# One PSUM buffer for all banks, a smaller copy of K, shared weight tiles, and sums of G written to PSUM, in a kernel that fuses attention with a gated MLP

## The chip, the cores and the metric

The kernel runs on one core of a Trainium2 chip. The metric is device time in microseconds (us) of one execution, lower is better. Engines: PE (TensorE), DVE (VectorE), ACT (ScalarE), POOL (GpSimd), and SP, which here only issues DMAs.

## The reference

```python
# q, k, v: 8 batches x 8 heads x 576 positions x 64;  tau = 0.02
scores = q @ k.T / sqrt(64)
scores = where(scores >= max(scores) - tau, scores, -1e9)
attn = exp(scores - max(scores));  attn = attn / sum(attn)
x = attn @ v                        # as 4608 tokens x 512
gate = sigmoid(x @ w_gate)          # w_gate, w_val: 512 x 1536
out = (gate * (x @ w_val)) @ w_out  # w_out: 1536 x 512
```

The scores decide by a threshold what counts, so they are computed in nearly full precision: each operand of a fast matmul (type fp32r) is split into a high part (rounded) and a low part (the rest), and the products high-high, high-low and low-high are summed in PSUM.

## The kernel before

**Planning.** The program is not written in the order in which it runs. It records operations with an engine, a cost, a key (the due time) and the buffers that they use; `Plan.run` then plays the record through with these costs and emits each operation when its engine, its inputs and its buffers are free, lowest key first. So a buffer count, a gate or a cost changes the order on all engines. Each engine executes its part strictly in order.

**Attention.** Heads are taken in pairs (a batch has four, 32 in all, numbered 0 to 31; `Visit`). A pair has nine score tiles of 128 queries by 576 keys: four for each head and one that holds the last 64 queries of both. For a tile (`tile_steps`), PE writes the scores to PSUM (L713, before pair 4 in plain fp32, L705), DVE takes the negative maximum (L721) and the threshold (L730), ACT the exponential (L735), and DVE masks and sums the row (L738); PE transposes the 576 columns (`tp` L819, `lk` L832), ACT copies them to SBUF (L771), and PE multiplies by V (`av`, L855). All reads of a score tile are from PSUM, so it is held from the scores to the mask.

**The score operands** (`split_scores`). K is split into `k2` (high and low). For each head `kd` is a copy by DMA of both parts, put once on the head's own 64 rows and once on the other 64; `qd` has the high part of Q on the own rows and the low part on the others. A tile is then two matmuls of 128 rows by halves of 288 keys: `qd` with kd's high part gives high-high and low-high, and `qd` with kd's low part gives high-low (and a negligible low-low).

**PSUM.** There are eight banks of 512 fp32 columns. Before pair 4 three score tiles of two banks and two single banks are in use. Once the MoE work has begun (`active["moe"]`), two score tiles keep four banks, and four single banks (`b`) serve transposes and `av` (at most two) and MoE sums (at most two).

**MoE.** Tokens are worked on in blocks of 512: blocks 0 to 7 are the first 512 positions of the batches, block 8 all the leftover positions. Blocks 0, 1 and 2 are multiplied directly, beside the attention of later batches (`in_units`): a unit is 12 matmuls of 512 columns (`m`, L938), 24 units a block, 72 in all. Units and pairs are tied to each other by `RATE` (2.7 units a pair from pair 4 on): a pair waits for a unit (`held_by`), and a unit for a pair. The weights of a unit, 512 KB, come from DRAM (`wi`), for each block anew. Meanwhile POOL forms sums of the weights (`in_sums`, `out_sums`). ACT (tanh) and DVE (L918) make G, the gated product, in two slabs of 512 tokens a tile. G of the blocks 2 and 6 goes to DRAM and comes back (`ga`, `gd`, `gb`).

**The tail.** After the attention come, in this order: the output stage of blocks 0, 1, 2; the input products of the block pairs 3-4 and 5-6 (`in_two`, seven products in place of eight, chains `qa`, `qb`, `qc` in PSUM, L1148); the output stage of blocks 3, 4, 5; the input products of 7-8; the output stage of 6, 7, 8. An output stage (`out_three`) multiplies a 3 by 3 grid of G (three parts of the 1536 features, three blocks) by the weights with 15 products of 24 matmuls (`oc`, L1222), 360 in all. `ORDER` gives the products' order, `G_STEPS` the sums of G that they need: ("n", d, x, y, sign) writes the sum of slabs x and y to d, ("c", r, x) splits slab x for product r. Each step is done for four columns. A sum is a DVE TENSOR_TENSOR of two SBUF slabs (L1009). A split (`halves_of`) is a rounded copy by ACT (`gt`, L1061) and a subtraction for the low part (L1064), by POOL, DVE, POOL in turn (`G_LOW`). The products' PSUM results are added up by ACT (L1243) and DVE (`oa`, L1247). The operands of the next input products (`xb`, `xs_p`) are made in the same way.

Of the kernel before, what the change touches and what calls it, by code (L numbers as in the profile page):

```python
# [46 lines left out]
class Plan:  # L47
# [3 lines left out]
    IN_TURN = ("x", "xf", "kn", "qn", "k2", "q2", "kd", "qd", "vs", "p", "pt", "pl", "ptc")  # L51
# [7 lines left out]
    def __init__(self, pools, slots):  # L59
# [5 lines left out]
        self.taken, self.now = {}, 0.0  # L65
# [4 lines left out]
    def make(self, b):  # L70
        if b.place is not None:
            at = min(b.place)
            tag = f"{b.tag}{at}"
            return self.bank_pool(tag).tile(b.shape, b.dtype, tag=tag, name=b.name, bufs=1)
# [38 lines left out]
    def room(self, o):  # L113
# [5 lines left out]
        for (tag, cls), s in need.items():  # L119
            own[tag] = own.get(tag, 0) + len(s)  # L120
        for (tag, cls), s in need.items():
            if tag in self.ANY:
                if sum(max(0, len(self.vacant[t]) - own.get(t, 0)) for t in self.homes_of(tag)) < len(s) + o.leave:
                    return False
                lines = {}
                for b in s:
                    if b.line is not None:
                        lines.setdefault(b.line, []).append(b.turn)
                if any(sorted(v) != list(range(self.given.get(k, 0) + 1, self.given.get(k, 0) + 1 + len(v)))
                       for k, v in lines.items()):  # L130
                    return False
                continue
# [33 lines left out]
    def settle(self, bufs):  # L166
# [3 lines left out]
        for b in bufs:  # L170
            if b.tag not in ("s", "b"):
                continue
            for at in self.homes(b.tag):
                if not taken & at:
                    places[b] = at
                    taken |= at
# [7 lines left out]
    def run(self):  # L184
# [10 lines left out]
        while True:  # L195
# [39 lines left out]
            while events and events[0][0] <= now + 1e-9:  # L235
# [5 lines left out]
                else:  # L241
                    for b in x.bufs:
                        b.users -= 1
                        if not b.users and b.held:
                            self.live.pop(b, None)
# [22 lines left out]
    "kn": 1, "qn": 1, "k2": 1, "q2": 1, "kd": 3, "qd": 3, "vs": 3,  # L268
    "p": 3, "pc": 1, "sm": 8, "st": 16, "pt": 4, "pl": 2, "ptc": 1, "plc": 1, "xf": 2, "rb": 1, "x": 6, "g": 12,
# [46 lines left out]
RATE, SLACK, LEAP = 2.7, 3, 5  # L316

def LATE(b, hp):
# [3 lines left out]
KD_COST = 1.2  # L322
# [3 lines left out]
SUMS_IN, SUM_KEY, SUM_OUT = {1: (0,), 2: (1,)}, 300, 290  # L326
# [5 lines left out]
G_LOW = ("POOL", "DVE", "POOL")  # L332
# [47 lines left out]
def kernel(  # L380
# [70 lines left out]
    ahead = ExitStack()  # L451
    ps_more = ahead.enter_context(tc.tile_pool(name="ps_more", bufs=1, space=PSUM))
    warm = ps.tile([P, 2, SM], F32, tag="s0", name="warm", bufs=1)
    for i in range(WARM):
        nc.tensor.matmul(
            warm[:, i % 2, :P], ident, ident, is_transpose=True, start=True, stop=True, skip_group_check=True
# [3 lines left out]
    pools["s"], pools["b"] = (ps, 3), (ps, 4)  # L460
# [3 lines left out]
    class Both(Plan):  # L464
        def cap(self, tag, cls):
            if tag == "s" and active["moe"]:
                return 2 if cls is None else None
# [6 lines left out]
            return 2 if active["att"] else 4  # L474

        def homes(self, tag):
            if tag == "s":
                return [{0, 1}, {2, 3}] + ([] if active["moe"] else [{4, 5}])
            return [{6}, {7}] + ([{4}, {5}] if active["moe"] else [])

        def bank_pool(self, tag):
            if tag == "s4":
# [469 lines left out]
    def streamed(blk, tag=""):  # L952
        return lambda f, i: stream(
            wi_d[f, i], lambda: wi_d[f, i].t.rearrange("p z c f -> p (z c f)"), f"wi{blk}_{f}_{i}{tag}"
        )

# [482 lines left out]
```

## Time and profile before

| | |
|---|---|
| median of 3 runs | 1462.29 us (1460.71 to 1463.02) |
| the profiled execution's own time | 1457.04 us |
| its span, first to last instruction | 1454.9 us |
| PE busy | 1341.3 us, 92% |
| DVE, ACT, POOL busy | 1065.1, 742.9, 618.7 us |
| mean granted PE clock | 0.97 |
| moved by DMA | 338.12 MB |

Columns of the views are named where they are shown. A group's row gives busy time and mean duration of its instructions, then the idle time of the engine just before them and what ended it. Names are those of the program, with buffer numbers left out; L1009 is line 1009 of the kernel.

### The profile page before, as it was taken

How to read it: one execution, taken by the hardware profiler on the slowest of the kernel's cores; microseconds unless marked ns; L12 is line 12 of the kernel's file. 1: busy time of each engine (PE TensorE's matmuls, PEld its weight loads, DVE VectorE, ACT ScalarE, POOL GpSimd, SP SyncE). 2: the span in 40 equal slices, each digit the busy share in tenths (PEclk: the TensorE clock that was granted, in tenths of full speed). 3: DMA queues.
4: the chain of work that ended last, by engine and by line, in shares of the span. 5: the costliest groups of instructions: out<-in, count | busy, mean ns of one | idle time of the engine just before them, and what ended most of it. 6: DMA issues, size and time to landing. Idle time of an engine off the chain costs nothing.

```text
span 1454.9 us, 23511 instructions
## 1 busy us (share of the span) xinstructions
PE 1341.3 (92%) x8184; PEld 1083.1 (74%) x8184; DVE 1065.1 (73%) x1936; ACT 742.9 (51%) x1375; POOL 618.7 (43%) x530
## 2 busy tenths in 40 slices
PE   8989999899999899999987979999999969999978
PEld 5568877787787677777765767888888758888757
DVE  7888778877777667677787887576546986456983
ACT  8787666667676666676655533132113434113431
POOL 3557222645634743655634565011001766001762
PEclk9999999999999899999988989999999989999989
DMA  8689668998988989999995338575666628676634
GB/s 319 197 247 334 195 189 277 266 307 239 282 231 240 273 269 275 269 289 265 312 296 156 111 127 298 193 249 195 220 224 214 218 90 311 199 254 222 196 95 151
DMA packets 137284, 338.12 MB, mean 232 GB/s; under 512 B 25040, under 2 KB 35536, under 8 KB 137168
## 3 DMA queue, kind: packets, MB, share of 16 engines
q1 hardware_dynamic: 137024, 336.64, 74.3%
q8 instruction: 65, 1.06, 0.3%
q14 instruction: 51, 0.42, 0.1%
q10 hardware_dynamic: 144, 0.00, 0.0%
HBM read 216.92 MB, written 68.27 MB: 196 GB/s over the span
## 4 chain that ended last, share of the span: by engine, by line
PE 64%; DVE 15%; DMA 9%; ACT 4%; issue 4%; SPq 2%; POOL 2%; DVEq 0%; POOLq 0%; ACTq 0%
PE m L938 11%; PE qb L1148 9%; PE av L855 8%; PE oc L1222 8%; PE qa L1148 7%; PE qc L1148 6%; PE s L713 6%; PE tp L819 6%; DVE g L1009 5%; DVE gt L1064 3%; DMA td<-wt 2%; DMA kd<-k 2%; DVE gb L1009 2%; DVE p L738 1%; PE s L705 1%
## 5 line engine op out<-in xcount | busy, mean ns | idle before, releaser
L1222 PE MATMUL oc<-gt,wo 128*128 128x512 f32 x1080 | 267.6, 408 | 37.2 <-DVE oa L1247 17.4
L1064 POOL TENSOR_TENSOR gt<-g,gt 128x512 fp32r<-128x512 f32 x97 | 152.6, 1597 | 306.3 <-ACT gt L1061 287.6
L1222 PEld LDWEIGHTS oc<-gt,wo 128*128 128x128 f32 x1080 | 211.3, 198 | 89.8 <-DVE oa L1247 21.6
L721 DVE TENSOR_REDUCE st<-s 128x1 f32<-128x576 f32 x256 | 192.5, 754 | 94.5 <-PE s L713 87.4
L738 DVE SCALAR_TENSOR_TENSOR p<-s,st,p 128x576 f32<-128x576 f32 x256 | 206.6, 812 | 33.7 <-ACT p L735 30.2
L735 ACT ACTIVATE p<-s,st 128x576 f32<-128x576 f32 x256 | 191.1, 750 | 52.0 <-DVE st L721 51.4
L713 PE MATMUL s<-kd,qd 128*128 128x288 f32 x896 | 173.1, 318 | 34.7 <-DVE p L738 27.4
L771 ACT COPY pt<-tp 128x512 f32<-128x512 f32 x256 | 148.5, 587 | 96.4 <-PE tp L819 92.6
L713 PEld LDWEIGHTS s<-kd,qd 128*128 128x128 f32 x896 | 136.9, 196 | 52.5 <-issue 20.9
L819 PE MATMUL tp<-ident,p 128*128 128x128 f32 x1024 | 162.4, 286 | 13.8 <-ACT pt L771 7.3
L938 PE MATMUL m<-x,wi 128*128 128x512 f32 x576 | 167.7, 408 | 2.3 <-DMA wi<-wid 1.7
L819 PEld LDWEIGHTS tp<-ident,p 128*128 128x128 f32 x1024 | 124.0, 145 | 44.5 <-ACT pt L771 11.1
L1061 ACT CAST gt<-g 128x512 fp32r<-128x512 f32 x144 | 82.9, 620 | 97.1 <-DVE g L1009 88.7
L855 PE MATMUL av<-pt,vs 128*64 128x256 f32 x1024 | 127.6, 392 | 1.2 <-ACT pt L771 1.2
L1148 PE MATMUL qa<-xs_p,wa 128*128 128x512 f32 x432 | 109.6, 389 | 0.0
L938 PEld LDWEIGHTS m<-x,wi 128*128 128x128 f32 x576 | 98.2, 190 | 14.3 <-DMA wi<-wid 1.9
L1100 DVE TENSOR_TENSOR qu<-qb,qp 128x512 f32<-128x512 f32 x72 | 49.7, 691 | 78.7 <-PE qb L1148 75.6
L855 PEld LDWEIGHTS av<-pt,vs 128*64 128x64 f32 x1024 | 69.3, 139 | 50.2 <-issue 11.4
L1148 PEld LDWEIGHTS qa<-xs_p,wa 128*128 128x128 f32 x432 | 81.1, 188 | 16.8
L1009 DVE TENSOR_TENSOR g<-g,g 128x512 f32<-128x512 f32 x96 | 89.9, 975 | 0.3
L1064 POOL TENSOR_TENSOR xs_p<-xb,xs_p 128x512 fp32r<-128x512 f32 x24 | 34.9, 1468 | 120.5 <-ACT xs_p L1061 120.5
L632 POOL TENSOR_TENSOR k<-kn,k 128x640 fp32r<-128x640 f32 x28 | 44.2, 1580 | 90.3 <-ACT k L628 65.4
(123 smaller groups left out, 2318.9 us busy)
## 6 DMA issues: line engine op xcount, KB each, us to landing
wo<-td SPq DMA_DIRECT2D x90, 512.0 KB
kd<-k SPq DMA_DIRECT2D x112, 320.0 KB
wi<-wid SPq DMA_DIRECT2D x48, 512.0 KB
wa<-wid SPq DMA_DIRECT2D x36, 512.0 KB
ws<-sid SPq DMA_DIRECT2D x36, 512.0 KB
wt<-sid SPq DMA_DIRECT2D x36, 512.0 KB
td<-wt SPq DMA_DIRECT2D x30, 512.0 KB
qd<-q SPq DMA_DIRECT2D x112, 128.0 KB
```

What stands on the lines that cost most here:

```text
L713: nc.tensor.matmul(s.ap[:, c, :HALF], st(), mv(slice(kc + c * HALF, kc + (c + 1) * HALF)), start=m == 0, stop=m == len(steps) - 1,)
L721: op("DVE", 0.76, key, lambda: nc.vector.tensor_reduce(out=st.ap[:, 0:1], in_=sv(), axis=AX.XY, op=ALU.max, negate=True), reads=[s], write ...
L735: op("ACT", 0.74, key, lambda: nc.scalar.activation(p(), sv(), AF.Exp, bias=st.ap[:, 0:1], scale=1.0), reads=[s, (st, 0)], writes=[(g.p, i)])
L738: op("DVE", 0.9, key, lambda: nc.vector.scalar_tensor_tensor(out=p(), in0=sv(), scalar=st.ap[:, 1:2], in1=p(), op0=ALU.is_ge, op1=ALU.mult ...
L771: return op("ACT", act(n), key, lambda: nc.scalar.copy(dst(), src.ap), reads=[src], writes=[part])
L819: nc.tensor.matmul(tp.ap[:, c, :], self.p.ap[:, o + c * P : o + (c + 1) * P], ident, is_transpose=True, start=c == 0, stop=c == NJ - 1, sk ...
L855: nc.tensor.matmul(av.ap[h * D : (h + 1) * D, a:z], vis.vs.ap[:, j, h], m(h), start=i == 0, stop=i == len(ms) - 1, skip_group_check=True,)
L938: nc.tensor.matmul(m.ap, wv[:, a, c * P : (c + 1) * P], xs[c].ap[:, z], start=e == 0, stop=e == 11,)
L1009: return op(e, cost, key, lambda: engine.tensor_tensor(out=out(), in0=a(), in1=b(), op=ALU.add if kind == "+" else ALU.subtract), reads=re ...
L1064: op(low, {"DVE": 0.69, "POOL": 1.3}[low], key, lambda: engine.tensor_tensor(out=to.ap[:, 1], in0=src.get(), in1=f32(to.ap[:, 0]), op=ALU. ...
L1148: nc.tensor.matmul(acc.ap, wv[:, y, (2 * h + c) * P : (2 * h + c + 1) * P], xt[prod][c].ap[:, z], start=e == 0 and prod in FIRST, stop=e = ...
L1222: nc.tensor.matmul(acc.get(), w.ap[:, a, y, e * P : (e + 1) * P], ft[y].ap[:, z], start=r == CHAINS[c][0] and h == 0 and m == 0, stop=h == ...
```

## The change

- **PSUM.** One tile of 4096 columns, `banks`, is the only PSUM buffer. A score tile is 576 columns in a row. From pair 4 on there are three places: columns 192 to 767, 768 to 1343 and 1760 to 2335. The first two meet in bank 1; together they take five banks, and three are left for single use, all eight once the attention is over. The score matmuls are cut where a tile crosses into its second bank: 320 and 256, 256 and 320, or 288 and 288 columns. Place and bank are chosen by how long they have been free. Before pair 4 three tiles have two banks each.
- **K.** `kh` and `kl` are separate buffers. Only `kh` is copied to `kd`, which has half the size. The product with the low part of K takes `kl` where POOL wrote it, against `qz`: four buffers whose other rows were set to zero at the start, and whose own rows get the high part of Q by one more DMA for each head.
- **Blocks 1 and 2** run in one series of units, after the attention of batch 2: each weight tile is loaded once and used for both. Pairs and units are tied by `units_by`: 3 units a pair up to pair 12, then 2.4.
- **Sums of G.** Six of the 13 sum steps become ("l", r, x, y, sign): DVE writes the sum to a PSUM bank, ACT rounds it from there, and DVE subtracts from there for the low part. The other nine splits get their low parts from POOL alone. The operand splits and the sums into PSUM wait for the last unit (`gate[1]`), as the splits did; in the first output stage the loads of block 2's G now do, too.
- **Buffers.** The sums of the chains and of the output stage are single banks. `x` has eight slots, G of blocks 2, 3 and 7 lies in other slots (`G_IN`), and `kd`, `vs` and `ptc` have moved to the other list of lendable slots.

```diff
-        "A": ("g", "x", "pt", "kd", "p", "k2", "q2", "vs", "ptc"),
-        "B": ("t2", "qd", "kn", "qn", "xf", "rb", "pc"),
+        "A": ("g", "x", "pt", "p", "q2"),
+        "B": ("t2", "qd", "kd", "kn", "qn", "xf", "rb", "pc", "qz", "kh", "kl", "ptc", "vs"),
...
-RATE, SLACK, LEAP = 2.7, 3, 5
+SLACK, LEAP = 3, 5
...
-G_LOW = ("POOL", "DVE", "POOL")
+G_LOW = ("POOL",)
...
-    (("c", 5, 6), ("n", 6, 1, 6, "-"), ("n", 6, 6, 3, "r"), ("c", 0, 6), ("n", 1, 1, 7, "-")),
+    (("c", 5, 6), ("n", 6, 1, 6, "-"), ("l", 0, 6, 3, "r"), ("n", 1, 1, 7, "-")),
...
+    banks = ps.tile([P, 8 * SM], F32, tag="banks", name="banks", bufs=1)
+    quarter = SM // 2
+    scores_at = {
+        None: {(0, 1): SM + quarter - S, (1.5, 2): SM + quarter, (3, 4): 4 * SM - HALF},
+        "plain": {(0, 1, 1.5): SM - HALF, (2, 3): 3 * SM - HALF, (4, 5): 5 * SM - HALF},
+    }
...
-            if tag == "s" and active["moe"]:
-                return 2 if cls is None else None
...
-            return 2 if active["att"] else 4
+            return 2 if active["att"] else None
...
+            late = not active["att"] and not any(x.tag == "s" for x in self.live)
+            return ([(0,), (1, 1.5), (2,), (3,), (4,)] if late else []) + [(5,), (6,), (7,)]
...
-                kd = self.kd[h] = buf("kd", [P, 2, SK], F32R, f"kd{n}_{h}")
+                kd = self.kd[h] = buf("kd", [P, SK], F32R, f"kd{n}_{h}")
+                qz = zero_rows[h, self.hp % 2]
...
-                        out=f32(kd.ap[rows]), in_=f32(k2.ap[own, :, :SK])
-                    ), reads=[k2], writes=[(kd, rows.start)])
+                        out=f32(kd.ap[rows]), in_=f32(kh.ap[own])
+                    ), reads=[kh], writes=[(kd, rows.start)])
+                op("SP", 0.5, key + h + 0.1, lambda qz=qz, own=own: nc.sync.dma_start(
+                    out=f32(qz.ap[own]), in_=f32(q2.ap[own, 0, :WM])
+                ), reads=[(q2, 0)], writes=[(qz, "own")])
...
-                (lambda: vis.qd[h].ap[:, cols], lambda c, z=z: vis.kd[h].ap[:, z, c]) for z in range(2)
+                (lambda: vis.qd[h].ap[:, cols], lambda c: vis.kd[h].ap[:, c]),
+                (lambda: qz.ap[:, cols], lambda c: vis.kl.ap[:, c]),
...
-                for c in range(2):
+                for a, z in ((0, s.border), (s.border, S)):
                     nc.tensor.matmul(
-                        s.ap[:, c, :HALF], st(), mv(slice(kc + c * HALF, kc + (c + 1) * HALF)),
-                        start=m == 0, stop=m == len(steps) - 1,
+                        s.ap[:, a:z], st(), mv(slice(kc + a, kc + z)),
+                        start=m == 0, stop=m == len(steps) - 1, skip_group_check=True,
                     )
...
+    def units_by(pair):
+        return 3 * (pair - 4) if pair <= 12 else 24 + 2.4 * (pair - 12)
...
+                for b in blks:
+                    m = buf("b", [P, SM], F32, f"m{b}_{f}_{i}", "moe")
...
-                    halves_of(now, entry(step[2], c), t, next(lows), after=gate[1])
+                    src, low = entry(step[2], c), "DVE"
+                    if step[0] == "l":
+                        x, y, m = src, entry(step[3], c), buf("b", [P, SM], F32, f"gm{n}_{r}_{c}", "moe", f"sums{n}")
+                        src = Part(m, lambda m=m: m.ap)
+                        combine("DVE", 0.69, now, src.get, x.get, y.get, step[4], [(z.b, z.part) for z in (x, y)], [m],
+                                gate[1])
+                    else:
+                        low = next(lows)
+                    halves_of(now, src, t, low, after=gate[1])
...
-    m = out_three(0, TRIPLES[0], 400, ([], [last]))
+    m = out_three(0, TRIPLES[0], 400, ([last], [last]))
```

More of the change, by code (lines that the diff above doesn't have):

```diff
@@ L120, in room @@
             own[tag] = own.get(tag, 0) + len(s)
+        lines = {}
+        for b in itertools.chain(*need.values()):
+            if b.line is not None:
+                lines.setdefault(b.line, []).append(b.turn)
+        for k, v in lines.items():
+            if sorted(v) != list(range(self.given.get(k, 0) + 1, self.given.get(k, 0) + 1 + len(v))):
+                return False
         for (tag, cls), s in need.items():
@@ L172, in settle @@
                 continue
-            for at in self.homes(b.tag):
-                if not taken & at:
+            for at in sorted(self.homes(b), key=lambda at: max(self.freed.get(x, 0.0) for x in at)):
+                if not taken & set(at):
                     places[b] = at
-                    taken |= at
+                    taken |= set(at)
                     break
@@ L578, in convert @@
         ), reads=[ws], writes=[wi_d[f, i]])
+    zero_rows = {}
+    for h, i in itertools.product(range(2), range(2)):
+        qz = zero_rows[h, i] = buf("qz", [P, SM], F32R, f"qz{h}_{i}")
+        rows = slice((1 - h) * D, (2 - h) * D)
+        op("ACT", act(SM), 1 + h + i, lambda qz=qz, rows=rows: nc.scalar.copy(
+            qz.ap[rows], zero_t[rows, 0:1].to_broadcast((D, SM))
+        ), writes=[(qz, "zero")])
     class Visit:
@@ L1003, in in_sums, with combine @@
         sums(f"{f}_{i}", u, v, lambda t, z: view(t)[:, z], lambda t, z, h: view(t)[:, z, 2 * h : 2 * h + 2], put)
-    def combine(e, cost, key, out, x, y, kind, reads, writes):
+    def combine(e, cost, key, out, x, y, kind, reads, writes, after=()):
         a, b = (y, x) if kind == "r" else (x, y)
@@ L1010, in combine @@
             out=out(), in0=a(), in1=b(), op=ALU.add if kind == "+" else ALU.subtract
-        ), reads=reads, writes=writes)
+        ), reads=reads, writes=writes, after=after)
     def out_sums(h, after):
@@ L1058, in halves_of @@
     def halves_of(key, src, to, low, leave=0, after=()):
-        rd = [(src.b, src.part)] if src.b is not to else []
-        op("ACT", act(SM), key, lambda: nc.scalar.copy(to.ap[:, 0], src.get()), reads=rd, writes=[(to, 0)] if rd else [to],
+        rd = [(src.b, src.part)]
+        op("ACT", act(SM), key, lambda: nc.scalar.copy(to.ap[:, 0], src.get()), reads=rd, writes=[(to, 0)],
            leave=leave, after=after)
@@ L1167, in out_three @@
             if b in AWAY_G:
-                gs[b] = {f: buf("A", [P, 2, SM], F32, f"gb{b}_{f}") for f in F1}
-                for f in F1:
-                    op("SP", 1.7, key, lambda b=b, f=f: nc.sync.dma_start(out=gs[b][f].ap, in_=gd_d[b, f].t),
-                       reads=[gd_d[b, f]], writes=[gs[b][f]], after=gate[0])
+                new_g(b, G_IN[b])
+                for f, z in itertools.product(F1, range(2)):
+                    g = slab(b, f, z)[0]
+                    op("SP", 1.0, key, lambda b=b, f=f, z=z, g=g: nc.sync.dma_start(out=g.get(), in_=gd_d[b, f].t[:, z]),
+                       reads=[(gd_d[b, f], z)], writes=[(g.b, g.part)], after=gate[0])
         def entry(x, c):
```

207 lines of the change are left out of this document (99 added, 108 removed), and 7 rows, old and new, of the table G_STEPS.

## The prediction

> **What bounds the kernel now.** I read the stretches first, cut at the stages' borders. Columns: stretch, its length, busy time (and instructions) of PE, PEld, DVE, ACT and POOL, then the granted clock, the DMA share and GB/s.
>
> ```profile
> 100.00:740.00 640.00, 601.09 (x4539) 494.57 (x4538) 486.92 (x1098) 426.99 (x809) 325.54 (x291) 0.98 0.91 268
> 740.00:780.00 40.00, 33.78 (x259) 27.52 (x260) 35.52 (x76) 21.73 (x38) 11.69 (x8) 0.87 0.89 270
> 780.00:900.00 120.00, 99.21 (x466) 77.79 (x467) 94.05 (x121) 51.25 (x92) 70.16 (x50) 0.93 0.46 156
> 900.00:1120.00 220.00, 220.00 (x973) 182.21 (x972) 127.14 (x183) 50.24 (x87) 14.84 (x10) 1.00 0.66 218
> 1120.00:1240.00 120.00, 104.65 (x435) 84.09 (x434) 99.55 (x112) 51.15 (x92) 77.47 (x48) 0.94 0.63 211
> 1240.00:1340.00 100.00, 100.00 (x443) 82.84 (x442) 54.58 (x80) 20.68 (x36) 1.16 (x1) 1.00 0.66 224
> 1340.00:1455.00 115.00, 95.96 (x396) 76.75 (x394) 85.24 (x96) 39.39 (x71) 64.55 (x40) 0.94 0.45 151
> ```
>
> Two stretches (900 to 1120, 1240 to 1340: the products for two blocks at a time) are full of PE at clock 1.00; nothing is to be won there. PE loses time in the attention (39 us idle of 640) and in the three output stages around 780 to 900, 1120 to 1240 and 1340 to 1455: 20.8, 15.4 and 19.0 us idle, and another 6 or 7 us each because the clock falls to 0.93 or 0.94 (99.21 by 0.07 is 6.9). In those three POOL and DVE are busy together, elsewhere in the tail POOL rests. So I asked for the groups between 1110 and 1240 (busy us, mean ns, then idle before and its releaser), and for the spread of the instructions on g (min/median/max ns).
>
> ```profile
> L1222 PE MATMUL oc<-gt,wo 128*128 128x512 f32 x360 | 88.1, 406 | 13.5 <-DVE oa L1247 7.3 <-ACT oa L1243 4.6 <-POOL gt L1064 1.6
> L1064 POOL TENSOR_TENSOR gt<-g,gt 128x512 fp32r<-128x512 f32 x40 | 66.1, 1682 | 131.0 <-ACT gt L1061 129.6 <-PE oc L1222 1.4
> L1064 DVE TENSOR_TENSOR gt<-g,gt 128x512 fp32r<-128x512 f32 x20 | 23.0, 1159 | 3.3 <-ACT gt L1061 3.2
> L1247 DVE SCALAR_TENSOR_TENSOR oa<-oc,oa 128x512 f32<-128x512 f32 x20 | 13.3, 681 | 8.0 <-PE oc L1222 8.0
> L1009 DVE TENSOR_TENSOR xb<-xb,xb 128x512 f32<-128x512 f32 x8 | 8.5, 1079 | 4.4 <-POOL xs_p L1064 4.3
> L1009 DVE TENSOR_TENSOR g<-g,g x47: 675/682/1783, 1115.4 to 1196.8; 128x512 f32<-128x512 f32 x47
> L1064 POOL TENSOR_TENSOR gt<-g,gt x40: 1267/1728/3408, 1121.2 to 1210.8; 128x512 fp32r<-128x512 f32 x40
> L1064 DVE TENSOR_TENSOR gt<-g,gt x20: 678/1156/1781, 1121.7 to 1206.3; 128x512 fp32r<-128x512 f32 x20
> ```
>
> A sum of two slabs of G takes 0.68 us bare and up to 1.78, a low part on POOL 1.27 bare and up to 3.41, while `oa`, which reads PSUM and one slab, stays at 0.681. The long ones are as long as the other engine's instruction on top of their own: DVE with two SBUF inputs and POOL take turns. Adding bare times as if nothing overlapped: 52 sums (13 steps of G_STEPS by 4 columns), 20 low parts on DVE, 8 sums of x and 6 low parts of x, 86 by 0.68 = 58.5; 40 + 8 on POOL by 1.27 = 61.0; together 119.5 us, and the stage from the first sum (1115.4) to 1235 lasts 120. So turn-taking, not PE, sets this stage: PE's matmuls, 435 by 0.227 us, would need 99.
>
> ```profile
> 929.04 2.72 PE qb L1148 x12
> 1406.41 44.08 PE oc L1222 x186
> ```
>
> 0.227 is the first of these rows of the chain of waits, 2.72 over 12. The second says that in the last stage the sums are done at 1406, and PE then works off a backlog to the end.
>
> **The change part by part.** The sum is made against the profiled execution, 1457.04 us (span 1454.9 and 2.1 around it). The median shown, 1462.29, is 5.25 higher; I add that at the end.
>
> *Sums of G by way of PSUM.* Six of the thirteen sum steps now write a PSUM bank, and the low parts of those six products are taken by DVE from that bank; POOL alone takes the other nine. On DVE, first output stage, before (g are slabs of G, gt the split operands):
>
> ```order
> L1064 TENSOR_TENSOR gt_5_3_10293<-g_9_2953,gt_5_3_10293 128x512
> L1009 TENSOR_TENSOR g_8_2753<-g_0_3819,g_8_2753 128x512
> L1009 TENSOR_TENSOR g_9_2953<-g_1_4245,g_9_2953 128x512
> L1009 TENSOR_TENSOR g_8_2753<-g_4_1962,g_8_2753 128x512
> L1009 TENSOR_TENSOR g_9_2953<-g_5_2051,g_9_2953 128x512
> ```
>
> After (banks is the one PSUM buffer):
>
> ```order
> L1027 TENSOR_TENSOR banks<-g_4_1874,g_8_2927 128x512
> L1027 TENSOR_TENSOR g_9_3172<-g_1_4687,g_9_3172 128x512
> L1027 TENSOR_TENSOR banks<-g_5_2149,g_9_3172 128x512
> L1027 TENSOR_TENSOR g_8_2927<-g_0_3650,g_8_2927 128x512
> L1082 TENSOR_TENSOR gt_0_0_9470<-banks,gt_0_0_9470 128x512
> ```
>
> The sums still read two slabs, so I leave all 52 in the turn-taking; no row of before has two SBUF inputs and a PSUM output, and the ends are 0.675 and 1.783, the g row's own. The 24 new low parts read PSUM and one slab, as the next row's does: 0.69 with no long ones in the mean, outside the turn-taking.
>
> ```profile
> L1100 DVE TENSOR_TENSOR qu<-qb,qp 128x512 f32<-128x512 f32 x72 | 49.7, 691 | 78.7 <-PE qb L1148 75.6 <-ACT g L915 2.5 <-DMA wt<-sid 0.6
> ```
>
> A stage loses 20 by 0.68 and 4 by 1.27 of turns, 13.6 + 5.1 = 18.7 us: 119.5 becomes 100.8, and PE's 99 is right behind. The Trainium skill, "SBUF — State Buffer", section "Who interferes with whom", says the same of the cause: a DVE instruction with two SBUF inputs and a GpSimd instruction that reads SBUF use one read interface, exclusively, and one with a single SBUF input does not; the 0.681 of `oa` agrees. By that rule alone a stage would get 18.7 back.
>
> Not all arrives. PE wants product 0 as its fifth, after 4 by 24 by 0.227 = 21.8 us, but its first low part now stands about 15th in DVE's queue, its last 24th; with the four products before it low-split on POOL (16 turns by 1.27 = 20.3, plus some 18 DVE turns by 0.68 = 12.2) it is whole only after some 32 us. In the two later stages POOL may start on the first products when the last unit's first product is done, some 8 us earlier (a unit is 42 by 0.227 = 9.5 us), which covers most of the 10 us between 32 and 21.8 but not all of it; where the new banks or the operand buffers are short, more is lost. I take 14 for the second stage and 12 for the third, where PE cannot finish before 396 by 0.227 = 90 of the 115 us; ends 0 and 19.
>
> *The end of the attention.* Units of the first MoE product were used up by pair 29, and the pairs 30 and 31 had parts of the output stage beside them. Before, on PE (tp transposes, s scores, oc output sums):
>
> ```order
> L713 MATMUL s_3_l_9854<-k_3_9664,q_3_9634 128x288 x6
> L819 MATMUL tp_2_120_9864<-ident,p_2_12_9840 128x128 x4
> L1222 MATMUL oc_0_9871<-gt_14_0_9556,wo_14_0_9233 128x512 x3
> L1222 MATMUL oc_0_9871<-gt_14_1_9571,wo_14_0_9233 128x512 x3
> L819 MATMUL tp_2_121_9888<-ident,p_2_12_9840 128x128 x4
> L832 MATMUL lk_2_12_9896<-ident,p_2_12_9840 128x128
> ```
>
> After, in the last pair:
>
> ```order
> L839 MATMUL banks<-ident,p_3_02_9073 128x128 x4
> L966 MATMUL banks<-x_0_2003,wi_11_1_8691 128x512 x2
> L839 MATMUL banks<-ident,p_3_02_9073 128x128 x4
> L852 MATMUL banks<-ident,p_3_02_9073 128x128
> L730 MATMUL banks<-kd_3_1_8817,qd_3_1_8814 128x288 x2
> ```
>
> The units now reach to the last pair, and all but one oc group follow the attention. From 740 to 900 PE lost 6.2 and 20.8 idle, 4.4 and 6.9 by the clock: 38 us. The units cover the first part (about 10); the output stage now starts with no sums done, 81 us of turns against PE's 360 by 0.227 = 82, and loses perhaps 28 with its start. I take 10 gained; ends 0 (all given back by the later start) and 20.
>
> *K's low part not copied, weights shared.*
>
> ```profile
> kd<-k SPq DMA_DIRECT2D x112, 320.0 KB
> wi<-wid SPq DMA_DIRECT2D x48, 512.0 KB
> qd<-q SPq DMA_DIRECT2D x112, 128.0 KB
> 260.00:280.00 20.00, 16.07 (x110) 13.21 (x110) 15.73 (x37) 13.26 (x27) 8.28 (x8) 0.83 1.00 284
> 480.00:500.00 20.00, 15.59 (x94) 12.79 (x92) 12.89 (x32) 10.54 (x19) 13.43 (x13) 0.83 1.06 255
> 520.00:540.00 20.00, 16.81 (x132) 13.34 (x132) 10.97 (x26) 12.38 (x24) 6.56 (x5) 0.91 0.83 266
> 560.00:580.00 20.00, 16.79 (x104) 14.36 (x102) 15.55 (x39) 13.06 (x26) 8.03 (x7) 1.00 0.98 283
> 256.02 5.24 DMA kd<-k
> 482.46 8.23 DMA wi<-wid
> ```
>
> kd falls to 160 KB (112 by 160 = 17.9 MB less), 56 copies of qd's size for the new zero-padded operand come in (7.2 MB), 24 of the 48 wi loads go (12.6 MB): 23 MB of some 170 (268 GB/s by 640 us), so the 0.91 share becomes about 0.79. The four worst slices lose 14.7 us idle and 7 by the clock, and transfers stand in the chain at two of them. I take 6 of these 22; ends 0 and 22. On SP's in-order queue the 56 new copies wait for PE to be done with the pair two before; kd and qd of the second head stand behind them, but that pair's scores are long past. Matmuls stay at four a tile. The gb loads of block 2 are now held until the last unit, which ends within the last pair: hidden behind its two av groups, one landing (5 us, as kd's above) if not. The low half of K now has two buffers, each held until its pair's last scores, which POOL waits for before it writes the pair after next; that is early enough as long as POOL is idle for half of the attention (325.5 of 640 us busy).
>
> *Three score tiles in five banks.* Score matmuls that wait for a tile to come free cost, by the waits of the whole span (us, times, longest),
>
> ```profile
> PE s L713 <- DVE p L738: 27.4, 23, 3.6
> L738 DVE SCALAR_TENSOR_TENSOR p<-s,st,p 128x576 f32<-128x576 f32 x256 | 206.6, 812 | 33.7 <-ACT p L735 30.2 <-issue 0.5 <-POOL st L730 0.4
> ```
>
> 27 us, at 23 of the 252 tiles of pairs 4 to 31 (9 a pair). A third tile can take up to 27 us of this away. But two of the three tiles share a bank, and the order then puts a second wait inside the tile. Before, then after, on PE with the waits:
>
> ```order
> L713 MATMUL s_1_l_5589<-k_1_5299,q_1_5323 128x288 [waits DVE_49]
> L713 MATMUL s_1_l_5589<-k_1_5299,q_1_5323 128x288
> L713 MATMUL s_1_l_5589<-k_1_5299,q_1_5323 128x288 [waits Pool_49]
> L713 MATMUL s_1_l_5589<-k_1_5299,q_1_5323 128x288 x3
> L819 MATMUL tp_1_000_5601<-ident,p_1_00_5562 128x128 [waits Activation_49]
> ```
>
> ```order
> L730 MATMUL banks<-kh_1_4738,q_1_4761 128x320 [waits DVE_49]
> L730 MATMUL banks<-kh_1_4738,q_1_4761 128x256 [waits DVE_49]
> L730 MATMUL banks<-kl_1_4769,q_1_4761 128x320
> L730 MATMUL banks<-kl_1_4769,q_1_4761 128x256
> L730 MATMUL banks<-kh_1_4738,q_1_4761 128x320
> ```
>
> The 256 columns lie in the neighbour's bank and wait for its latest read; transposes, av and units queue behind. If, as before, one wait in ten stalls PE for 1.2 us, 168 such tiles cost 20 us; the other end is rival A. Also one bank less serves transposes, av and units (three for four). I take nil for all of this; ends -27 and +68.
>
> The sum: 14 + 12 + 10 + 6 = 42 us, 1457 - 42 = 1415; on the footing of the medians **1420 us**. 0.2% (3 us) is about what a measurement of this kernel can tell from no change.
>
> **The rivals.**
>
> *A, slower: the shared bank.* If every second of the 168 tiles holds PE for one read of its neighbour (0.81 us, the row of L738 above), the attention grows by 84 by 0.81 = 68: 1420 + 68 = 1488. It decides from 42 / 0.81 = 52 stalled tiles on. For it: the reads of both tiles are also put in turn on DVE and ACT. Against: only 23 stalls in 252 now, PE is the late engine, DVE idles 24% of the attention. The Trainium skill, "PSUM — Partial Sum Buffer", section "PSUM bank collisions raise a hardware error", says why there is no way around these waits: PE's write and a read, or two engines' reads, must not meet in one bank, whatever the columns. No trace of before can show its price, since no two tiles shared a bank. Chance 0.14.
>
> *B, little: the turns remain.* The sums into PSUM keep POOL waiting, nine products in line on POOL alone (36 by 1.68, the mean above, is 60 us, the first five 34 against PE's 27) set the pace; the two later stages give 4 each, the first 0: 6 + 8 = 14, 1448. For it: POOL's mean now; against: 20 turns fewer on DVE leave less to wait for. Chance 0.23.
>
> *C, more: every bound is reached.* 19 and 20 in the later stages, 20 at the end of the attention, 10 by DMA: 69, so 1393. Chance 0.15.
>
> That the change does not do what it says, a third tile that is only nominal, is in the nil above.
>
> **How the numbers follow.** My forecast has 0.48. The range, 1394 to 1457, holds it and B, and half of C; it leaves out A. Faster by over 0.2%: the forecast, B and C, less a little of B that a part of A would eat: 0.84; within 0.2%: 0.03; slower: 0.13.
>
> **What would show it.** Right: in the stretches around the output stages the low parts from PSUM near 0.69 us, POOL's mean below 1.5, PE idle below 10 us a stage; PE busy to the last pair; DMA share near 0.8 in the attention. Wrong: score matmuls waiting for another tile's read for more than 40 us in all (A), POOL's low parts still near 1.7 and PE waiting for gt by POOL (B), an attention that ends later than before.

## The result and the profile after

| | before | after |
|---|---|---|
| median | 1462.59 us (4 runs) | 1385.26 us (4 runs, 1382.40 to 1387.76) |
| the profiled execution's own time | 1457.04 us | 1387.76 us |
| its span | 1454.9 us | 1385.9 us |

After by before is 0.9473, 95% interval 0.9453 to 0.9493: 77 us faster, where 42 were forecast, and 9 us below the range. The page of after, with the slices of PE and of its granted clock, then the chain of waits by engine, then two groups of the output stages:

```profile
PE 1329.1 (96%) x8184; PEld 1063.8 (77%) x8184; DVE 1033.4 (75%) x1948; ACT 741.9 (54%) x1379; POOL 586.8 (42%) x518
PE   8889999999999999999999999999999999999998
PEclk9899999999999999999999999999999999999999
PE 63%; DVE 21%; ACT 7%; POOL 4%; issue 4%; DMA 2%; SPq 0%; DVEq 0%; ACTq 0%; POOLq 0%
L1082 POOL TENSOR_TENSOR gt<-g,gt 128x512 fp32r<-128x512 f32 x108 | 161.9, 1532 | 283.9 <-ACT gt L1079 282.6
L1244 PE MATMUL banks<-gt,wo 128*128 128x512 f32 x1080 | 251.7, 394 | 9.3 <-DVE gt L1082 7.5
```

The hollows of PE are gone, in the attention and in the output stages, and so are most of those of the clock (0.96 is left in the first output stage). The stretches of after that answer to those of before: the attention from the first unit to the last `av`, then the three output stages (columns as in the prediction).

```profile
100.80:774.00 673.20, 646.88 (x4938) 519.29 (x4938) 521.19 (x1205) 460.69 (x868) 340.40 (x305) 1.00 0.75 232
773.90:861.30 87.40, 83.58 (x364) 68.33 (x359) 77.02 (x94) 39.68 (x74) 56.60 (x38) 0.96 0.68 234
1091.00:1179.60 88.60, 85.85 (x373) 69.37 (x372) 80.82 (x101) 40.41 (x74) 57.74 (x38) 1.00 0.67 233
1294.10:1385.90 91.80, 85.70 (x373) 69.28 (x371) 71.95 (x96) 34.10 (x63) 47.01 (x32) 0.99 0.52 177
```

PE idles 3.8, 2.8 and 6.1 us in the three stages. To see where the 69 us between the two profiled executions went, I cut each at the input products, which nothing disturbs. The row of one product (its fastest, median and slowest matmul in ns, then first and last start) gives the first border, in before and in after:

```profile
L1148 PE MATMUL qa<-xs_p,wa x432: 389/389/389, 901.7 to 1343.5; 128*128 128x512 f32 x144
```

```profile
L1166 PE MATMUL banks<-xs_p,wa x432: 388/389/397, 861.3 to 1292.5; 128*128 128x512 f32 x144
```

The same cut for all kernels, in us. "Start" is the time of the first two-block product, so all of the attention with the first output stage; "second" and "third" are the later output stages, from the last matmul of one group of input products to the first of the next, or to the end.

| kernel | start | second | third | span |
|---|---|---|---|---|
| before | 901.7 | 98.3 | 102.0 | 1454.9 |
| after | 861.3 | 82.9 | 86.1 | 1385.9 |
| e1 two tiles | 861.8 | 83.0 | 86.1 | 1382.5 |
| e2 traffic | 916.5 | 83.0 | 86.1 | 1439.9 |
| e3 old pacing | 865.1 | 82.9 | 86.1 | 1388.5 |
| e4 sums in SBUF | 868.8 | 92.8 | 89.3 | 1399.7 |
| e5 weights twice | 886.2 | 82.9 | 86.1 | 1409.9 |
| e6 K copies | 873.5 | 82.9 | 86.2 | 1397.0 |
| e7 before, less traffic | 877.0 | 98.2 | 101.4 | 1431.4 |
| e8 old sums | 876.6 | 98.1 | 95.8 | 1425.0 |
| e9 weight bytes | 875.1 | 82.9 | 86.2 | 1395.9 |
| e10 e7, new pacing | 877.8 | 98.3 | 102.1 | 1431.1 |
| e11 two tiles, slower units | 879.1 | 83.3 | 86.2 | 1400.2 |
| e12 before, K low not copied | 889.9 | 98.2 | 102.5 | 1443.4 |
| e13 equal traffic | 909.5 | 83.0 | 86.2 | 1433.0 |
| e14 equal traffic, old sums | 913.5 | 99.6 | 95.1 | 1461.1 |
| e15 eight weight buffers | 881.3 | 82.9 | 86.2 | 1404.7 |
| e16, e17 ten weight buffers | 877.3, 874.4 | 82.9, 82.8 | 86.2, 86.2 | 1400.6, 1397.8 |
| e18 the same, two tiles | 866.0 | 82.8 | 86.2 | 1386.6 |

After against before: 40.4 at the start, 15.4 and 15.9 in the two later stages, less 2.7 in the products between: 69.0. The later stages came out near the forecast (14 and 12). The start was forecast at 16 (10 for the end of the attention, 6 for the transfers); it gave 40. The experiments ask what the other 24 are.

### The profile page after: what moved, and what is told of

Same layout as the page of the kernel before. It is cut to its first block, busy times and chain, and to the rows that moved or that the text cites. A ratio compares the mean times of both kernels' runs of the same rounds, so it can differ in the third digit from the quotient of the medians.

```text
span 1385.9 us, 23622 instructions
## 1 busy us (share of the span) xinstructions
PE 1329.1 (96%) x8184; PEld 1063.8 (77%) x8184; DVE 1033.4 (75%) x1948; ACT 741.9 (54%) x1379; POOL 586.8 (42%) x518
## 4 chain that ended last, share of the span: by engine, by line
PE 63%; DVE 21%; ACT 7%; POOL 4%; issue 4%; DMA 2%; SPq 0%; DVEq 0%; ACTq 0%; POOLq 0%
PE banks L1166 24%; PE banks L966 10%; PE banks L730 9%; PE banks L875 8%; PE banks L839 6%; PE banks L1244 5%; DVE p L755 4%; DVE st L738 4%; POOL gt L1082 3%; ACT p L752 3%; DVE banks L1027 3%; DVE g L1027 2%; DVE gt L1082 2%; DVE oa L1269 2%; PE banks L721 1%
## 5 line engine op out<-in xcount | busy, mean ns | idle before, releaser
L1244 PE MATMUL banks<-gt,wo 128*128 128x512 f32 x1080 | 251.7, 394 | 9.3 <-DVE gt L1082 7.5
L738 DVE TENSOR_REDUCE st<-banks 128x1 f32<-128x576 f32 x256 | 191.9, 752 | 83.9 <-PE banks L730 45.6
L1244 PEld LDWEIGHTS banks<-gt,wo 128*128 128x128 f32 x1080 | 203.6, 189 | 56.2 <-DVE gt L1082 11.5
L755 DVE SCALAR_TENSOR_TENSOR p<-banks,st,p 128x576 f32<-128x576 f32 x256 | 206.2, 813 | 52.3 <-ACT p L752 29.0
L752 ACT ACTIVATE p<-banks,st 128x576 f32<-128x576 f32 x256 | 187.6, 746 | 81.5 <-DVE st L738 37.1
L788 ACT COPY pt<-banks 128x512 f32<-128x512 f32 x256 | 147.1, 588 | 67.1 <-PE banks L839 63.6
L966 PE MATMUL banks<-x,wi 128*128 128x512 f32 x576 | 170.6, 410 | 2.0 <-ACT g L942 1.1
L839 PE MATMUL banks<-ident,p 128*128 128x128 f32 x1024 | 153.4, 278 | 5.2 <-ACT pt L788 1.6
L839 PEld LDWEIGHTS banks<-ident,p 128*128 128x128 f32 x1024 | 121.1, 142 | 34.9 <-issue 6.7
L875 PE MATMUL banks<-pt,vs 128*64 128x256 f32 x1024 | 126.3, 389 | 0.4 <-ACT pt L788 0.4
```

The source lines that it names most:

```text
L738: op("DVE", 0.76, key, lambda: nc.vector.tensor_reduce(out=st.ap[:, 0:1], in_=sv(), axis=AX.X, op=ALU.max, negate=True), reads=[s], writes ...
L752: op("ACT", 0.74, key, lambda: nc.scalar.activation(p(), sv(), AF.Exp, bias=st.ap[:, 0:1], scale=1.0), reads=[s, (st, 0)], writes=[(g.p, i)])
L755: op("DVE", 0.9, key, lambda: nc.vector.scalar_tensor_tensor(out=p(), in0=sv(), scalar=st.ap[:, 1:2], in1=p(), op0=ALU.is_ge, op1=ALU.mult ...
L788: return op("ACT", act(n), key, lambda: nc.scalar.copy(dst(), src.ap), reads=[src], writes=[part])
L839: nc.tensor.matmul(tp.ap[:, c, :], self.p.ap[:, o + c * P : o + (c + 1) * P], ident, is_transpose=True, start=c == 0, stop=c == NJ - 1, sk ...
L875: nc.tensor.matmul(av.ap[h * D : (h + 1) * D, a:z], vis.vs.ap[:, j, h], m(h), start=i == 0, stop=i == len(ms) - 1, skip_group_check=True,)
```

## The experiments

The theories for the start. T1: transfers removed. T2: the third score tile. T3: the new pacing. And, beside them, that the sums of G gain in the first output stage as in the later two, for which my sum had no term of its own. One caution holds throughout: the order is planned anew for each kernel, so an edit can move instructions far away from it. Three kernels are clean of that, by the instructions of each engine in order of time, alike neighbours taken together and buffer numbers left out: in e12 none of a computing engine stands elsewhere than in before, in e4 none of PE elsewhere than in after, and in e8 1932 of the 1937 groups that PE has in after stand in the same order.

### The third score tile (e1, e11)

```diff
-        None: {(0, 1): SM + quarter - S, (1.5, 2): SM + quarter, (3, 4): 4 * SM - HALF},
+        None: {(0, 1): SM - HALF, (2, 3): 3 * SM - HALF},
```

and bank 4 for single use once the MoE runs.

> After with two score tiles in the attention in place of three: the banks are laid out as before the change (two tiles of two banks each, none shared, four single banks once the products of the MoE run). If the third score tile brings most of the attention's unforecast 35 us (theory T2), 1405 to 1420 us against after's 1385, and score matmuls wait for DVE's p by some 25 us again. If the traffic (T1) or the new pacing of the units (T3) brings it, 1380 to 1390. If the shared bank costs more than the third tile brings (my rival A in small), under 1380.

Measured: 1386.25 us, 0.9489 of before (0.9457 to 0.9521); after is at 0.9473. No difference. PE's waits for the mask in e1, and in after (us, times, longest, over the attention):

```profile
PE banks L731 <- DVE p L756: 31.0, 30, 2.3
```

```profile
PE banks L730 <- DVE p L755: 9.1, 24, 1.1
PE banks L730 <- DVE st L738: 4.9, 12, 0.9
PE banks L730 <- ACT p L752: 3.2, 10, 0.4
```

The third tile does take 22 us of long waits away, and the shared bank brings some 8 us of short ones (on `st` and `p` of the neighbour). The rest comes back elsewhere: with two tiles and one more bank the units run ahead, and 48 of the 360 matmuls of the first output stage are done before the last `av` (6 in after). T2 falls as a gain in sum. Would two tiles with the units held back be better than both? The edit is `LEAP` from 5 to 1.

> After with two score tiles, as in the run that came to 1386, and a unit allowed to run at most one ahead of the pacing in place of five. With two tiles the units ran ahead (used up at 720, last av at 789) and PE idled 10 us after that. If the shared bank's waits in after cost what the third tile brings, two tiles with the units spread to the end are a little better than both: 1374 to 1382. If units running ahead are harmless: 1384 to 1390. If they are needed to fill PE's waits: over 1390.

Measured: 1409.28 us, 23 over e1. With two tiles, units that run ahead are needed: the start comes 17 us later than in e1, in a profiled execution that was the fastest of the four by 7.

### The pacing (e3, e10)

```diff
-        return 3 * (pair - 4) if pair <= 12 else 24 + 2.4 * (pair - 12)
+        return 2.7 * (pair - 4)
```

> After with the units of the first MoE product asked for at 2.7 a pair throughout, as before the change, in place of 3 a pair up to pair 12 and 2.4 from there. If the pacing brings the gain at the end of the attention (T3; my term of 10), the units end about two pairs before the last and the time is 1395 to 1405; if the pacing matters for the whole attention, up to 1420; if neither, 1383 to 1388.

Measured: 1390.71 us, 5 over after; the start 3.8 later, the last unit still at 764. T3 has at most these 5. The new pacing in before (with less traffic, e7 below):

> The run of before with 24.2 MB less traffic (1434, output not the reference's for the same reason), and the units paced as after: 3 a pair up to pair 12, then 2.4. In that run the units are used up at 697 and the last av comes at 787. My term for the end of the attention was 10: 1420 to 1427 if it holds there; old pacing in after cost 5, which would give 1427 to 1431. If this reaches what after with the old sums has (1425), the attention is explained by traffic and pacing without the new layout of PSUM; if it stays at 1432 or above, the layout has a share.

Measured: 1433.57 us, as without it (1433.75). Nothing there.

### The sums of G (e4, e8)

Only where the six sums are written (the order on PE stays as it was):

```diff
-  ... buf("b", [P, SM], F32, f"gm{n}_{r}_{c}", "moe", f"sums{n}")
+  ... buf("B", [P, SM], F32, f"gm{n}_{r}_{c}", line=f"sums{n}")
```

> After with the six last sums of a block of G written to SBUF and not to PSUM; DVE still takes the six low parts, now from two SBUF inputs. The 24 low parts of a stage then go back into the turn-taking with POOL: by my prediction's terms 24 by 0.68 = 16 us more turns a stage, so 1385 + 14 + 12 and some of the first stage, 1411 to 1430, and the low parts on DVE with a mean near 1.1 us in place of 0.678. If where the sums are written is immaterial (the gain coming from the attention alone), 1385 to 1390.

Measured: 1401.58 us, 16 over after. The low parts on DVE and the sums, in e4 and in after (min/median/max ns):

```profile
L1082 DVE TENSOR_TENSOR gt<-gm,gt x72: 672/682/1780, 795.7 to 1384.3; 128x512 fp32r<-128x512 f32 x72
L1027 DVE TENSOR_TENSOR gm<-g,g x72: 677/681/1791, 791.2 to 1376.1; 128x512 f32<-128x512 f32 x72
```

```profile
L1082 DVE TENSOR_TENSOR gt<-banks,gt x72: 673/678/699, 798.4 to 1368.8; 128x512 fp32r<-128x512 f32 x72
L1027 DVE TENSOR_TENSOR banks<-g,g x72: 683/699/1795, 793.7 to 1363.1; 128x512 f32<-128x512 f32 x72
```

From PSUM no low part takes over 0.699 us, from SBUF up to 1.78. The sums take up to 1.79 either way, since they read two slabs: writing to PSUM does not take an instruction out of the turn-taking, reading from it does. The start comes 7.5 later, the second stage takes 9.9 more, the third 3.2. Undoing all of this part:

```diff
-G_LOW = ("POOL",)
+G_LOW = ("POOL", "DVE", "POOL")
```

and `G_STEPS` as before.

> After with the old table of the sums of G and the old dealing of the low parts: all thirteen sums to SBUF, low parts by POOL, DVE, POOL in turn. The traces of before and after differ by 17.5 and 18 us in the second and third output stage; if all of that is this part's, and the first stage loses as in the run with sums in SBUF (10) or more, 1385 + 45 = 1420 to 1440. If half of it comes from the banks (five free ones in place of four), 1402 to 1415.

Measured: 1425.23 us, 40 over after: 15.3 at the start, 15.2 in the second stage, 9.7 in the third. So, on top of the rest of the change, this part is worth the same in the first output stage as in the second. Of the third stage's gain of 15.9, 6.2 stay with the old sums; e14 below, which has nothing of the change but layout and pacing, shows about the same there (95.1, 6.9 less than before).

### The transfers (e2, e5, e6, e7, e12, e13)

Put back into after, as load (K's copies go to DRAM here, those of before went to SBUF): weight tiles loaded for each block (`w = held[f, i] = weights(f, i, b)` inside the loop over blocks), and

```diff
+  kx = dram([D, SK], f"kx{n}_{h}_{rows.start}")
+  op("SP", KD_COST, key + h, lambda kx=kx, own=own: nc.sync.dma_start(
+      out=kx.t, in_=f32(self.kl.ap[own])
+  ), reads=[self.kl], writes=[kx])
```

> After with the removed transfers put back as load on the queues: the weight tiles of blocks 1 and 2 are loaded anew for each block, and K's low part is copied by as many transfers of the same bytes into a scratch in DRAM that nothing reads. If DMA relief brings most of the attention's 35 us (T1), 1405 to 1420 us and a DMA share near 0.9 between 100 and 740; if it is the third tile (T2) or the pacing (T3), 1385 to 1392 with that same share. My prediction's own term was 6, so 1391.

Measured: 1436.00 us, 51 over after, the start 55 later. More than any of the theories had asked for; the DMA share from 100 to 740 rose from 0.76 to 0.85. These are 7 MB more than the change takes away net (`qz` stays), so once more with exactly the net bytes (K's copies cut to 384 columns):

> After with the weight tiles loaded anew for each of blocks 1 and 2 (12.6 MB) and K's low part copied in 384 of its 640 columns (10.8 MB) into a scratch that nothing reads: 23.4 MB, what the change takes away net. The runs with 12.6 and with 30.5 MB gave +27 and +51. If the costs add by kind (27 for the tiles, 11 by 10.8/17.9 = 7 for the copies), 1385 + 34 = 1419; if the two kinds get in each other's way, up to 1432; under 1412 if the load of the queues does not matter beyond the tiles.

Measured: 1435.49 us, 0.9827 (0.9790 to 0.9864). The bytes of K's copies hardly mattered; the number of packets (145719) is that of e2. Each kind alone:

> After with the weight tiles of blocks 1 and 2 loaded anew for each of the two blocks (24 loads of 512 KB, 12.6 MB, put back); K's low part is not copied. The run with 12.6 and 17.9 MB put back together came to 1436, 50 us over after. If the loss goes with the bytes, this gives 50 by 12.6/30.5 = 21 us, 1401 to 1411. If transfers only cost once the queues are nearly full (a threshold), under 8 us, 1385 to 1393. If it is the place of K's copies in the queue and not their bytes, also under 8 us, and the next run shows nearly all of the 50.

Measured: 1412.14 us, 27 over after.

> After with only K's low part copied (112 transfers of 160 KB, 17.9 MB, into a scratch in DRAM that nothing reads); weights shared. By bytes: 50 by 17.9/30.5 = 29 us, 1409 to 1420. By a threshold: under 15 us, 1385 to 1400. By the place in the queue (the copies wait there for POOL's low part, and what stands behind them waits too): 40 us or more, 1425 to 1440.

Measured: 1396.56 us, 11 over after. Neither goes by bytes: 2.1 us a MB for the weights, 0.6 for K's copies (18.4 MB by the DMA totals of the pages, where I had reckoned 17.9). Nor do they add: 27 and 11 alone, 50 together in e13, with fewer bytes of K. The other direction, before with less:

```diff
-  out=f32(kd.ap[rows]), in_=f32(k2.ap[own, :, :SK])
+  out=f32(kd.ap[rows, 0]), in_=f32(k2.ap[own, 0, :SK])
...
+  again = blk in (1, 2) and f not in F1 and i not in SUMS_IN[blk]
-  w = held[f, i] = weights(f, i)
+  w = held[f, i] = held[f - 2, i] if again else weights(f, i)
```

> Before with less traffic and nothing else: K's low part is not copied (17.9 MB less; the second product of the scores then reads the high part again, so the output isn't the reference's), and 12 of the 48 weight tiles of blocks 1 and 2 are not loaded, the tile of the column before being used in their place (6.3 MB less). 24.2 MB less in all, about what the change takes away net (23.6 MB). Two score tiles, four banks, old pacing, old sums. If traffic makes the attention's gain (T1), 30 to 40 us off before's 1460: 1420 to 1430, DMA share near 0.8 and the last av before 790. If the gain needs the new layout or pacing as well, 1445 to 1458.

Measured: 1433.75 us, 0.9810 (0.9783 to 0.9836), 28 off before. The start comes at 877.0, 24.7 earlier than in before; the later stages do not move. So T1 holds in both directions, if each time in an order that is planned anew. And the first edit of the two alone (the second product of the scores reads K's high part again), where every engine's instructions stand as in before and only the copies are smaller:

> Before with K's low part not copied alone (17.9 MB less, the second product of the scores reads the high part again, so the output isn't the reference's); all 48 weight tiles are loaded. Both removed gave 28 us off 1461. By bytes, 28 by 17.9/24.2 = 21: 1438 to 1443. If weights cost more for their bytes, as in after (27 us for 12.6 MB against 11 us for 17.9 MB), 8 to 14 us: 1447 to 1453.

Measured: 1444.72 us, 0.9911 (0.9877 to 0.9945): 12 to 13 us, all at the start.

```profile
L1148 PE MATMUL qa<-xs_p,wa x432: 389/389/389, 889.9 to 1331.5; 128*128 128x512 f32 x144
```

The chain of waits says what changed. Between 96 and 740 us of before it stands on 17 transfers of over 2 us, 106 us in all; some of them (start, us):

```profile
274.74 5.43 DMA rd<-turned
286.62 7.25 DMA kd<-k
295.23 5.65 DMA kd<-k
...
435.25 9.49 DMA kd<-k
...
464.98 7.65 DMA td<-wt
...
491.85 8.18 DMA td<-wt
...
515.45 6.74 DMA td<-wt
...
661.02 8.29 DMA qd<-q
...
680.09 6.23 DMA wi<-wid
...
690.71 6.56 DMA kn<-in_k_dram
```

In the same stretch of e12 these two are all of that kind, 8 us, and in after these four, 18 us:

```profile
511.05 4.76 DMA td<-wt
...
584.97 3.72 DMA td<-wt
```

```profile
293.99 7.26 DMA kd<-kh
301.27 5.08 DMA wi<-wid
...
357.38 2.64 DMA qz<-q
...
543.82 3.16 DMA gd<-ga
```

With 18.4 MB less of K's copies, transfers of other things, too, left the chain: sums of weights (`td`), Q, K. That took 98 us off the chain and gave 12: where a transfer no longer bounds, the engines' own work is close behind. A transfer's length in the chain is no measure of its price.

### Bytes or buffers (e9, e15 to e18)

Why do 12.6 MB of weights cost 27 us? The same bytes at the same place of the queue, into a scratch, so that no weight buffer is taken:

> After with the bytes of the second loading of the weights of blocks 1 and 2 and nothing else of it: behind each of the 24 loads stands, at the same place of the queue, one more transfer of 512 KB from DRAM to a scratch in DRAM. Loading the tiles twice gave +27 us over after's 1385; here no buffer for a weight tile is taken. If the bytes or the place in the queue cost the 27: 1406 to 1416. If it is the buffers of the weight tiles (nine, shared with the sums of the weights, so that loads come later and POOL's work on the sums is pushed together): 1385 to 1395.

Measured: 1396.82 us, 12 over after (by the ratio, 0.9581, it is 16). About half. One of the nine weight buffers (`"w": 9`) taken away and nothing else:

> After with eight buffers for weight tiles in place of nine and nothing else. If the second loading of the weights cost 15 of its 27 us by taking buffers from the sums of the weights and from loads ahead, one buffer less costs 5 to 20 us here: 1390 to 1405. If buffers were never short, 1383 to 1388, and the 15 lie in the order of the loads alone.

Measured: 1405.96 us, 21 over after. The sums of the weights, which POOL makes from the tiles in these buffers, go on for longer; their rows, with the start of the last one, in after, in e5 and in e15:

```profile
L996 POOL TENSOR_TENSOR s<-wi x24: 1270/1284/1859, 287.4 to 720.9; 128x512 f32<-128x512 f32 x24
```

```profile
L996 POOL TENSOR_TENSOR s<-wi x24: 1264/1284/1955, 290.4 to 766.6; 128x512 f32<-128x512 f32 x24
```

```profile
L996 POOL TENSOR_TENSOR s<-wi x24: 1268/1288/1891, 301.6 to 768.4; 128x512 f32<-128x512 f32 x24
```

46 and 48 us later. But that is no sign of missing buffers: in e9 and e6, which take no weight buffer, the last of these starts at 759.2 and 763.9. Would a tenth buffer be faster than both kernels? It was paid for with a buffer of `pt` (e16), with one of `t2` and one of `kl` (e17), and, with two score tiles, again with `pt` (e18).

> After with ten buffers for weight tiles, paid for with one of the four buffers of the transposed weights pt. If nine were still short: 1372 to 1382. If nine is enough and pt's fourth is not missed: 1383 to 1388. If pt's fourth is needed: over 1390.

> After with ten buffers for weight tiles, paid for with one of the six small ones (t2) and one of the two of K's low half. If nine were still short: 1372 to 1382. If K's low half needs its two buffers, since it is now held until its pair's last scores: over 1390, and POOL's kl waits for PE. Else 1383 to 1388.

> Ten buffers for weight tiles and three for pt, with two score tiles in the attention. With nine and four, two tiles came to 1386, their units far ahead of the pacing. If buffers hold the units back and units ahead fill PE's waits: 1370 to 1380, below both; if not, 1384 to 1392.

Measured: 1404.91, 1400.98 and 1388.52 us. None beats after, and the first two lose 16 to 20. That is also a warning for e5, e9 and e15: another pacing number, or one or two small buffers in exchange, cost 5 to 23 us here (e3, e11 against e1, e16, e17), by the new order or by what they take, so the split of the 27 us into bytes and buffers is not settled by them.

### What is left of the change (e14)

e13 with the old sums as well; only the layout of PSUM and the pacing remain.

> The same with the old table of the sums of G and the old dealing of the low parts as well: of the change only the layout of PSUM (three score tiles in five banks, five free banks in the output stages) and the pacing are left. If the three terms add, this stands at before less about 9: 1448 to 1456, 0.990 to 0.996 of it. If the layout and pacing bring nothing, 1457 to 1463. If the terms overlap (a stage that starts late hides the sums), under 1445.

Measured: 1459.92 us, 1.0006 of before (0.9984 to 1.0028). Layout and pacing together bring nothing that can be measured. By the profiled executions that nil is a sum: the start comes 11.8 later than in before (5 or more of it because e14's execution lies above its median and before's below), the third stage is 6.9 shorter. Going back to the old sums costs 24 us from e13, 40 from after (e8): the parts overlap. In e13 the start gains only 4.0 by the new sums, where after gains 15.3. The chain of waits of e13 at the begin of its first output stage shows what stands there beside the sums of G, sums of the weights (`s`), the last of which starts at 733.5 in after:

```profile
818.53 2.52 POOL s L1012 x2
821.05 12.45 POOL gt L1086 x10
```

That it is these that hide the new sums' gain was not tried.

## Why the prediction was wrong

- **What bounds the kernel.** Right. PE idled where I said, and the two stretches full of PE are as long as before (to 2.7 us).
- **Sums of G, 14 and 12.** Right: 15.4 and 15.9 measured, of which 15.2 and 9.7 go with the sums (e8). The 24 low parts take 0.678 as I had it (0.69). The Trainium skill, "SBUF — State Buffer", section "Who interferes with whom", holds for both halves: the low part with one SBUF input stays under 0.70, the sums with two reach 1.795 although they write PSUM. I expected POOL's mean below 1.5; it is 1.532, and the median, 1.728, is that of before's second stage: POOL still stands against the 52 sums.
- **The end of the attention, 10.** Mis-sized. The 81 us of turns in this term already counted the new sums, but I still let the stage lose 28 of the 38 us with its start. From 740 us to the first two-block product, in before, in e8 (old sums) and in after:

```profile
740.00:901.70 161.70, 134.70 (x732) 106.70 (x733) 129.57 (x196) 72.98 (x129) 81.86 (x58) 0.92 0.57 187
740.00:876.60 136.60, 120.83 (x611) 95.25 (x610) 120.68 (x155) 62.20 (x112) 87.67 (x58) 0.94 0.56 190
740.00:861.30 121.30, 117.25 (x632) 94.65 (x631) 103.38 (x155) 61.42 (x112) 72.13 (x52) 0.97 0.64 218
```

Idle time, and busy time by what the clock lacks, are 27.0 and 10.8 us, then 15.8 and 7.2, then 4.1 and 3.5. So 7.6 stayed where I had put 28, and between e8 and after 15.4 go, as the start comes 15.3 earlier by the sums. e3 shows about 4 for the pacing.

- **K's low part and the weights: "I take 6 of these 22".** This is the step that failed. At the start it measured 11.8 for K's copies alone with the order untouched (e12), 24.7 with 12 weight loads left out as well (e7), and 48.2 when both are put back into after (e13 against after); the last two were planned anew. How the 40.4 at the start divide depends on what is taken first. From before over e7 and e8 to after it is 24.7 for transfers, 0.4 for layout, pacing and the rest, 15.3 for the sums. Over e14 and e13 it is 11.8 lost by layout and pacing, 4.0 for the sums, 48.2 for transfers. Either way the transfers are the largest part. Two faults lay in my 6. I took the loss of the four worst slices (14.7 idle and 7 by the clock) for the upper end, while 17 transfers stood in the chain over the whole attention, 11 of them wholly outside those four slices. And I looked only at transfers of the kinds removed (`kd`, `wi`); 11 of the 17 are of other kinds, and in e12 only two of over 2 us are left, both `td`.
- **Three score tiles in five banks: nil.** Right as a sum (e1), in part by luck: the two terms I let cancel were 22 us of waits less and 8 of short ones more, and the other 14 do not show in the time: the units of e1 run ahead, and with these held back (e11) two tiles are 23 slower. Rival A, the shared bank, did not come: from 100 to 774 us the score matmuls wait 17.2 us for mask, maximum and exponential together, none over 1.1. The Trainium skill, "PSUM — Partial Sum Buffer", section "PSUM bank collisions raise a hardware error", has two engines' accesses to one bank kept apart even where their columns differ. This trace gives a price for two tiles that meet in a bank: the waits for the maximum and the exponential, 8.1 us in 22 waits, which e1 with its unshared tiles does not show.
- **Rival B** (14 us) fell with the stages. Of its two signs one came, POOL's low parts still near 1.7, and the other did not: before the output products PE idled 9.3 us in all, 7.5 of them for a low part by DVE. **Rival C**, every bound reached, was the nearest at 69: the stages (15 and 16 for its 19 and 20) came out below its terms, the transfers (25 for its 10) above.
- **The footing.** I added 5.25 us to stand on the medians. After's profiled execution lies 2.5 above its median instead: 8 of the 35 us that the forecast missed are no mechanism.

What stays open: how the part of the transfers beyond e12's 12 us divides into bytes, buffers and the order that the planner happens to find, why the transfers cost twice as much in after (48) as they gave in before (25), and whether layout or pacing gives the 6 or 7 us of the third stage.

## What to carry to other kernels

Where the chain of waits stands on many transfers, spread over a stage with DMA shares around 0.9, price removed traffic by a kernel that leaves the transfer out with the order unchanged, not by the idle time of the worst slices; here it was 12 us for 18.4 MB, where I had 6 for all. Where parts of a change overlap, say from which side a part was measured: the same sums were worth 15 us at the start in one kernel and 4 in another. Ask of each stage by itself whether a gain applies: the first output stage was of the same kind as the other two and stood only as a remainder in another term. In a planned kernel, a change of one buffer or one pacing number moved the whole order and cost up to 23 us here; keep an experiment's order the same, or count that much as scatter.

## What the runs showed of the hardware

- A DVE sum of two SBUF slabs that writes PSUM takes part in POOL's turns as one that writes SBUF: median 0.699, longest 1.795 (0.681 and 1.791 in e4).
- The granted clock of PE fell where PE idled: between 470 and 530 us of before, PE was busy 50.75 of 60 us at 0.89; in after 59.16 at 1.00. The Trainium skill, "TensorE: Matmul & The Clock Gate", section "Part 1: The HAM clock gate (the "warmup" mystery)", says that the gate follows how busy PE has been; these rows agree. Not every gap brings a fall: from 560 to 580 us of before PE was busy 16.79 of 20 us at 1.00.

```profile
470.00:500.00 30.00, 25.59 (x181) 21.03 (x181) 19.46 (x47) 17.35 (x32) 21.32 (x20) 0.89 1.03 283
500.00:530.00 30.00, 25.16 (x175) 19.96 (x174) 16.56 (x37) 19.39 (x38) 21.23 (x18) 0.89 0.94 295
```

```profile
470.00:500.00 30.00, 29.16 (x222) 23.53 (x222) 22.33 (x50) 21.77 (x42) 21.10 (x20) 1.00 0.93 293
500.00:530.00 30.00, 30.00 (x257) 24.67 (x254) 22.64 (x50) 21.29 (x41) 16.53 (x15) 1.00 0.88 286
```

The DMA moved as much there in after (293 and 286 GB/s) as in before (283 and 295): transfers at that rate do not by themselves make PE idle.
